# Test loads issued by GpSimd, and stores of weight sums and loads of down weights some steps later, in a two-layer FNet and GLU kernel

## The chip, the cores and the metric

The kernel runs on one core of a Trainium2 chip. The metric is the device time of one launch in microseconds. The core's engines work side by side, each through its own instructions in order: TensorE (PE in the profile; its weight loads are PEld), VectorE (DVE), ScalarE (ACT), GpSimd (POOL) and SyncE (SP), which here only issues transfers between the chip's memory (HBM) and the core's on-chip memory (SBUF).

## The reference

Two layers; each adds a Fourier mixing of the normalized rows and then a gated unit (GLU) of the normalized rows. x is 2048 rows of 640; the gate and up weights are 640 x 1728, the down weights 1728 x 640; all float32.

```python
def _A_ref(x, dft_seq_re, dft_seq_im, dft_hid_re, dft_hid_im):
    a = jnp.einsum("bsd,ed->bse", x, dft_hid_re)
    b = jnp.einsum("bsd,ed->bse", x, dft_hid_im)
    y = jnp.einsum("ts,bse->bte", dft_seq_re, a) - jnp.einsum("ts,bse->bte", dft_seq_im, b)
    return y

def _B_ref(x, w_gate, w_up, w_down):
    g = jnp.einsum("bsd,df->bsf", x, w_gate)
    u = jnp.einsum("bsd,df->bsf", x, w_up)
    h = _sigmoid(g) * u
    return jnp.einsum("bsf,fd->bsd", h, w_down)

x = A_x
x = x + _A_ref(_layernorm(x, axis=-1), A_dft_seq_re, A_dft_seq_im, A_dft_hid_re, A_dft_hid_im)
x = x + _B_ref(_layernorm(x, axis=-1), B_w_gate, B_w_up, B_w_down)
x = x + _A_ref(_layernorm(x, axis=-1), A_dft_seq_re, A_dft_seq_im, A_dft_hid_re, A_dft_hid_im)
x = x + _B_ref(_layernorm(x, axis=-1), B_w_gate, B_w_up, B_w_down)
```

The four Fourier matrices are inputs.

## The kernel before

**Numbers and memory.** x stays in SBUF, in one big tile (`big`) that also holds everything else. Operands of the matmuls are pairs of float16 parts: a high half, written by ScalarE (`split`, L236), and a low half, what the high half leaves, written by VectorE (L238). A product is three float16 products. Room in `big` is handed out by a planner (`take`) when the program is built; a new tile that lies where an old one lay waits on the chip until the old one has been read.

**Stages.** An opening does the first layer's Fourier mixing, which uses the mirror symmetry of the Fourier matrices. The GLU then takes the 2048 rows in four blocks of 512 (b = 0 to 3), each in steps: 14 steps j = 0 to 13 of gate and up products (13 tiles of 128 columns and a tail), and 8 steps of down products (`down`, L1242).

- Block 0 multiplies straight on (`gate_up`, 30 matmuls of 128x512 a step, L1049). In layer 1 its weights w(0,j) (gate), w(1,j) (up) and w(2,j) (down) arrive from HBM (`load_w`, L954 and L956), are split (`split_w`), and are kept in HBM as float16 pairs (`keep_w`, tensors kept_w, store at L254) for later use. ScalarE takes a step's result by a sigmoid (L1063), VectorE multiplies (L1064) into a tile `hf`, and a step later the result is split into halves (`gated_parts`, L1073 and L1074).
- Blocks 1 to 3 use seven smaller products in place of eight (`seven`, L1095). These need four sums of parts of the gate and up weights, s1 to s4: GpSimd adds them from the raw weights (`make_sums`, L998 to L1001), and `split_sums` makes the halves and stores them (tensors kept_s, through `keep` at L254). For 3 <= j < 13 both tiles of the sums lie in two fixed places that take turns. Later blocks load them with `load_s` (L1020 to L1023).

In layer 1, while block 1 to 3 run, the results of each block are folded for the second layer's mixing: statistics on VectorE (L415, L416), a power and scales on GpSimd (L398 to L411, L606 to L633), whose results ScalarE applies (L621, L623). Also in block 0, VectorE and GpSimd add the last of the mixing to x (`add_hidden`: L940 on VectorE, and one copy on GpSimd, L938).

**Tests.** The shortcuts hold only if the Fourier matrices have the symmetry, so the kernel tests it: beside layer 1's blocks 1 to 3 and layer 2's blocks 0 to 2 it loads all of the matrices in pieces, combines mirrored rows and columns on VectorE (`test_rows`, L1297 to L1300, and its like), and sums the squares of what is left on ScalarE (`square_rest`, L1275). At the end a flag chooses between this result and a general path. Each layer has 42 such tests of the large matrix, 32 of rows with four loads of 128 KB each (`load_rows`, L1291) and 10 of columns with two loads of 256 KB each (`load_cols`, L1308); layer 2 has 8 more of the small one, with two loads each (`load_hidden_rows`, L1351). The pieces use two rooms by turns, so a load waits until the test before last has been squared.

**Order.** The order is written by hand. `at(u, job)` puts a job into step u; the jobs of a step are emitted in order of u ahead of the step's matmuls, and each engine, SyncE's and GpSimd's transfers included, works strictly through what was emitted to it. So an instruction that waits holds up all behind it on its engine. In layer 1 block b starts at step `block[b]` = -3, 19, 41, 63. SyncE issues nearly all transfers and has at most eight under way; only the result's rows are stored by GpSimd (L378). Nothing but the order of emission says which of the waiting stores and loads goes first.

Of the kernel before, what the change touches and what calls it, by code (L numbers as in the profile page):

```python
# [16 lines left out]
P = 128  # L17
S = 2048
D = 640
F = 1728  # L20
NS = S // P
ND = D // P
# [7 lines left out]
HS = S // 2  # L30
# [148 lines left out]
@with_exitstack  # L179
def kernel(ctx: ExitStack, tc: tile.TileContext, x, ct, wh, wg, wu, wc, wd, out):  # L180
    nc = tc.nc
    pool = ctx.enter_context(tc.tile_pool(name="sb", bufs=1))
    psum = ctx.enter_context(tc.tile_pool(name="ps", bufs=1, space=bass.MemoryType.PSUM))
    dram = ctx.enter_context(tc.tile_pool(name="dr", bufs=1, space=bass.MemoryType.DRAM))

    big = pool.tile([P, (UNITS + 2 * CK) * UNIT], F32, name="big")
    acc = [psum.tile([P, 512], F32, name=f"acc{i}") for i in range(6)]
    flag = pool.tile([P, 1], I32, name="flag")
    with tc.manual_schedule():
        folded(ctx, tc, pool, dram, big, acc, flag, x, ct, wh, wg, wu, wc, wd, out)  # L190
    bad = nc.values_load(flag[0:1, 0:1], min_val=0, max_val=1,
                         skip_runtime_bounds_check_because="it is the result of a comparison")
    with tc.If(bad != 0):
        with tc.manual_schedule():
            general(tc, big, [acc[2 * i : 2 * i + 2] for i in range(4)], x, ct, wh, wg, wu, wc, wd, out)


def folded(ctx, tc, pool, dram, big, acc, flag, x, ct, wh, wg, wu, wc, wd, out):
    nc = tc.nc
# [33 lines left out]
    def split(dh, dl, src, s, do=ALL):  # L233

        if 0 in do:
            nc.scalar.activation(dh, src, AF.Copy, scale=s)  # L236
        if 1 in do:
            nc.vector.scalar_tensor_tensor(dl, src, s, dh, op0=OP.mult, op1=OP.subtract)  # L238
# [13 lines left out]
    def keep(v, *key):  # L252
        kept[key] = dram.tile(list(v.shape), F16, name="kept_" + "_".join(map(str, key)))
        nc.sync.dma_start(kept[key], v)  # L254
# [5 lines left out]
    def at(u, f, *a):  # L260
        jobs[max(0, int(u // 1))].append((u, f, a))

    held = {}
# [16 lines left out]
    def drop(*key):  # L280
        s = held.pop(key if len(key) > 1 else key[0])
        if s.span:
            slots.give(s)
# [703 lines left out]
    def take_sums(key, j):  # L987

        if 3 <= j < NF:
            return fixed(XU + XTU + 16 * (j % 2) + 8 * (key == "sp"), 8, key, j)  # L990
        return take(8, key, j)
# [13 lines left out]
    def split_sums(j, do):  # L1005
        v, w = held["sf", j].f32, take_sums("sp", j) if 0 in do else held["sp", j]
        h, l = w.parts
        for c, sign in ((slice(0, 256), -WS), (slice(256, 1024), WS)):
            split(h[:, c], l[:, c], v[:, c], sign, do)
        if 1 not in do:  # L1010
            return
        drop("sf", j)
        keep(w.f16, "s", j)
        if j < 3:
            held["S", j] = held.pop(("sp", j))
        else:
            drop("sp", j)

    def load_s(j):
        nc.sync.dma_start(take(5, "G", j).f16, kept["w", 0, j])  # L1020
# [261 lines left out]
    def room(k, n=CK):  # L1282
        u = UNITS + CK * (k % 2)
        return big[:, u * UNIT : (u + n) * UNIT]

    def load_rows(r, k):

        v = room(k).rearrange("p (g n c) -> p g n c", g=4, n=2)
        s = 1 + 16 * k
        for g, (row, d) in enumerate(((s, 1), (S - s, -1), (HS - s, -1), (HS + s, 1))):  # L1290
            nc.sync.dma_start(v[:, g], bass.AP(ct.tensor, (r * S + row) * S, [[P, NS], [d * S, 16], [1, P]]))  # L1291

    def test_rows(r, k):
        v = room(k)
# [8 lines left out]
    def load_cols(r, i, k):  # L1303

        n, row = (P, START[i]) if i < NB else (1, SB)
        v = room(k).rearrange("p (g c) -> p g c", g=4)[:n]
        for g, t in ((0, 1 + 256 * k), (2, HS - 256 * (k + 1))):
            nc.sync.dma_start(v[:, g : g + 2], bass.AP(ct.tensor, (r * S + row) * S + t, [[2 * S, n], [HS, 2], [1, 256]]))  # L1308

    def test_cols(r, i, k):  # L1310
        v = room(k)[: P if i < NB else 1]
# [35 lines left out]
    def load_hidden_rows(r, k):  # L1347

        v = room(k)[: 20 * ND].rearrange("p (g n c) -> p g n c", g=2, c=P)
        for g, (row, d) in enumerate(((1 + 80 * k, 1), (D - 1 - 80 * k, -1))):  # L1350
            nc.sync.dma_start(v[:, g], bass.AP(wh.tensor, (r * D + row) * D, [[P, ND], [d * D, 80], [1, P]]))  # L1351

    def test_hidden_rows(r, k):
        a, b = (room(k)[: 20 * ND, 4 * P * g : 4 * P * (g + 1)] for g in range(2))
# [112 lines left out]
    for layer in range(2):  # L1467
# [10 lines left out]
        block = []  # L1478
# [23 lines left out]
        if first:  # L1502
            for b in range(NB):
# [12 lines left out]
                else:  # L1516
                    for k in range(2):
                        v = d0 + 4 * k
# [41 lines left out]
        for b in range(1, NB):  # L1560
            for i in range(2):
                u = block[b] - 8 + 1.2 * i
# [9 lines left out]
        for b in range(NB):  # L1572
            for j in range(NF + 1):
                for q in ((0, j), (1, j)) if j < NF else ((3, 0),):
                    u = block[b] + j
# [12 lines left out]
            at(block[0] + j + (1.6 if j > 2 else 1.3), gated_parts, j)  # L1588
        for j in range(NF + 1):
            if first:  # L1590
                at(block[0] + 0.8 * j - 0.5, load_w, 2, j)
                at(block[0] + 0.8 * j + 1.6, split_w, 2, j)
                at(block[0] + j + 4, keep_w, 2, j)
            else:
                at(block[0] + j, load_w_again, 2, j)
                at(block[1] + j - 0.3, test_w, 2, j)

        if first:
            for j in range(NF):
                if 3 <= j < NF:  # L1600
                    u = block[0] + j - 1.5
                else:
                    u = block[1] - 8 + 1.5 * j
                    at(u - 2, load_sums, j)
                at(u, make_sums, j)
                at(u + 1.55, split_sums, j, (0,))
                at(u + 1.9, split_sums, j, (1,))
            at(block[0] + 12, close_slots)


# [2 lines left out]
        else:  # L1613
            u0, u1 = block[0] + 8, block[2] + 14
        tests = [(load_rows, test_rows, (layer, k)) for k in range(2 * NS)]
        tests += [(load_cols, test_cols, (layer, i, k)) for i in range(NB + 1) for k in range(2)]

        pace = (u1 - u0) / len(tests)
        for q, (load, test, key) in enumerate(tests):
            u = u0 + pace * q  # L1620
# [5 lines left out]
        if not first:  # L1626
            tests = [(load_hidden_rows, test_hidden_rows, (r, k), 15.5 + 1.7 * (4 * r + k), 2.8) for r in range(2)
                     for k in range(4)]
            tests += [(load_hidden_cols, test_hidden_cols, (r, j), 29.8 + 0.9 * (3 * r + j), 1.4) for r in range(2)
                      for j in range(3)]  # L1630
            for load, test, key, u, later in tests:
                at(block[2] + u, load, *key)
                at(block[2] + u + later, test, *key)
                at(block[2] + u + 1.15 * later, square_rest)
            at(block[3] + 16, test_all)
# [171 lines left out]
```

## Time and profile before

| | us |
|---|---|
| median of 3 runs | 1168.69 (1167.34 to 1170.28) |
| profiled execution, its own time | 1166.17 |
| its span | 1164.4 |
| TensorE busy in the span | 1128.2 |
| VectorE busy | 738.8 |
| ScalarE busy | 508.0 |
| GpSimd busy | 149.5 |
| mean granted clock of TensorE | 0.995 of full speed |

The span runs from the first to the last instruction; 1.77 us of the profiled execution lie around it. Rows of the profile name a line of the kernel, an engine, an operation and what it writes and reads (out<-in); "x30" counts instructions that stand together, and a bracket such as [1.84 <-DVE big L238] is the idle time ahead of the row and the instruction that ended it. Rows of SPq are transfers as SyncE issues them.

### The profile page before, as it was taken

How to read it: one execution, taken by the hardware profiler on the slowest of the kernel's cores; microseconds unless marked ns; L12 is line 12 of the kernel's file. 1: busy time of each engine (PE TensorE's matmuls, PEld its weight loads, DVE VectorE, ACT ScalarE, POOL GpSimd, SP SyncE). 2: the span in 40 equal slices, each digit the busy share in tenths (PEclk: the TensorE clock that was granted, in tenths of full speed). 3: DMA queues.
4: the chain of work that ended last, by engine and by line, in shares of the span. 5: the costliest groups of instructions: out<-in, count | busy, mean ns of one | idle time of the engine just before them, and what ended most of it. 6: DMA issues, size and time to landing. Idle time of an engine off the chain costs nothing.

```text
span 1164.4 us, 22633 instructions
## 1 busy us (share of the span) xinstructions
PE 1128.2 (97%) x8784; PEld 859.6 (74%) x8784; DVE 738.8 (63%) x1636; ACT 508.0 (44%) x1094; POOL 149.5 (13%) x269
## 2 busy tenths in 40 slices
PE   5699999999999999999999999999999999999997
PEld 2467346788878887888776844678887888788875
DVE  7996698668656776676427566746974557524530
ACT  6865474155524653365304422315552455225420
POOL 2312486110001010100000001000000001000000
PEclk9999999999999999999999999999999999999998
DMA  9417698849595977769305442787849683667301
GB/s 275 138 46 231 228 350 295 240 136 262 160 240 149 263 211 192 220 222 253 94 1 169 169 129 67 197 236 229 253 148 243 223 268 133 139 211 236 121 18 38
DMA packets 225621, 216.40 MB, mean 186 GB/s; under 512 B 68034, under 2 KB 181851, under 8 KB 225502
## 3 DMA queue, kind: packets, MB, share of 16 engines
q1 hardware_dynamic: 224862, 212.23, 61.5%
q0 software_dynamic: 640, 2.62, 0.6%
q8 instruction: 71, 1.16, 0.4%
q14 instruction: 48, 0.39, 0.1%
HBM read 171.03 MB, written 30.40 MB: 173 GB/s over the span
## 4 chain that ended last, share of the span: by engine, by line
PE 93%; DVE 3%; DMA 2%; POOL 1%; SPq 1%; ACT 0%; issue 0%; DVEq 0%; POOLq 0%
PE acc L1095 40%; PE acc L1242 31%; PE acc L1049 14%; PE acc L855 4%; PE acc L1178 2%; PE acc L773 2%; DVE big L238 1%; DMA big<-in_ct 1%; DMA big<-in_x 1%; DMA big<-in_wh 1%; PE acc L523 0%; DMA big<-in_wd 0%; POOL quad L372 0%; DVE big L627 0%; DVE big L664 0%
## 5 line engine op out<-in xcount | busy, mean ns | idle before, releaser
L1095 PE MATMUL acc<-big 128*128 128x256 f16 x4212 | 463.1, 273 | 0.1
L1095 PEld LDWEIGHTS <-big 128*128 128x128 f16 x4212 | 412.0, 98 | 48.6 <-DMA big<-kept_w 0.3
L1242 PE MATMUL acc<-big 128*128 128x320 f16 x2624 | 357.7, 299 | 0.0
L1242 PEld LDWEIGHTS <-big 128*128 128x128 f16 x2624 | 256.7, 98 | 99.7
L1099 ACT ACTIVATE big<-acc 128x256 f32<-128x256 f32 x312 | 116.6, 381 | 208.8 <-PE acc L1095 207.4
L1049 PE MATMUL acc<-big 128*128 128x512 f16 (+1 forms) x990 | 178.1, 342 | 4.6 <-DVE big L238 4.6
L1049 PEld LDWEIGHTS <-big 128*128 128x128 f16 x990 | 96.9, 98 | 84.9 <-DVE big L238 5.6
L1275 ACT ACTIVATE big<-big 128x768 f32<-128x768 f32 (+8 forms) x104 | 79.4, 764 | 124.9 <-DVE big L1300 91.2
L1163 DVE TENSOR_TENSOR big<-big 128x512 f16<-128x512 f32 x78 | 53.8, 690 | 109.2 <-ACT big L1162 109.2
L1257 DVE SCALAR_TENSOR_TENSOR big<-acc,big 128x320 f32<-128x320 f32 x64 | 28.4, 484 | 93.5 <-PE acc L1242 93.4
L238 DVE SCALAR_TENSOR_TENSOR big<-big 128x640 f16<-128x640 f32 (+6 forms) x81 | 64.9, 842 | 0.5 <-ACT big L236 0.4
L1141 ACT ACTIVATE big<-big 128x512 f32<-128x512 f32 x78 | 47.8, 627 | 37.2 <-DVE big L1132 36.9
L1297 DVE TENSOR_TENSOR big<-big 128x256 f32<-128x256 f32 x64 | 26.6, 416 | 49.8 <-DMA big<-in_ct 49.8
L1132 DVE TENSOR_TENSOR big<-big,acc 128x512 f32<-128x512 f32 x78 | 53.1, 681 | 4.2 <-PE acc L1095 4.0
L1151 DVE SCALAR_TENSOR_TENSOR big<-acc,big 128x256 f32<-128x256 f32 x78 | 32.6, 418 | 35.1 <-PE acc L1095 30.8
L236 ACT ACTIVATE big<-big 128x640 f16<-128x640 f32 (+7 forms) x81 | 49.6, 664 | 6.7 <-POOL big L998 4.3
L1162 ACT ACTIVATE big<-big 128x512 f16<-128x512 f32 x78 | 48.8, 625 | 6.5 <-DVE big L1153 5.6
L855 PE MATMUL acc<-big 128*128 128x321 f16 (+3 forms) x324 | 49.0, 300 | 1.1 <-DVE big L238 1.1
L1064 DVE SCALAR_TENSOR_TENSOR big<-acc,big 128x512 f32<-128x512 f32 x26 | 17.9, 687 | 40.4 <-PE acc L1049 28.5
L855 PEld LDWEIGHTS <-big 128*128 128x128 f16 (+3 forms) x324 | 28.2, 95 | 20.3 <-issue 7.7
L509 ACT ACTIVATE big<-big 128x384 f16<-128x384 f32 (+2 forms) x48 | 28.9, 647 | 31.0 <-DVE big L491 26.7
L1063 ACT ACTIVATE big<-acc 128x512 f32<-128x512 f32 x26 | 15.4, 592 | 57.6 <-DVE big L1074 27.2
(183 smaller groups left out, 1001.5 us busy)
## 6 DMA issues: line engine op xcount, KB each, us to landing
big<-kept_w SPq DMA_DIRECT2D x125, 320.0 KB
big<-kept_s SPq DMA_DIRECT2D x75, 512.0 KB
big<-in_ct SPq DMA_DIRECT2D x256, 128.0 KB
big<-kept_w SPq DMA_DIRECT2D x78, 192.0 KB
kept_w<-big SPq DMA_DIRECT2D x41, 320.0 KB
big<-in_ct SPq DMA_DIRECT2D x32, 256.0 KB
kept_s<-big SPq DMA_DIRECT2D x13, 512.0 KB
big<-in_wg SPq DMA_DIRECT2D x16, 320.0 KB
```

The costliest lines, as they stand in the source:

```text
L236: nc.scalar.activation(dh, src, AF.Copy, scale=s)
L238: nc.vector.scalar_tensor_tensor(dl, src, s, dh, op0=OP.mult, op1=OP.subtract)
L855: nc.tensor.matmul(ps[:m, :EC], z[:, at : at + m], w[:, 384 * wp : 384 * wp + EC], start=(d == 0 and zp == HI and wp == HI), stop=(d == ND ...
L1049: nc.tensor.matmul(ps, w[wp][:, d * P : (d + 1) * P], xt[:, xp, :], start=(d == 0 and wp == HI and xp == HI), stop=(d == ND - 1 and wp == LO))
L1095: nc.tensor.matmul(ps, wt, xt, start=start and n == 0, stop=n == len(todo) - 1, skip_group_check=not start)
L1099: nc.scalar.activation(dst, ps, AF.Copy)
L1132: nc.vector.tensor_tensor(v, v, other, op=OP.add)
L1141: nc.scalar.activation(v, v, AF.Sigmoid, scale=SG)
L1162: nc.scalar.activation(s.parts[HI], v, AF.Copy)
L1163: nc.vector.tensor_tensor(s.parts[LO], v, s.parts[HI], op=OP.subtract)
L1242: nc.tensor.matmul(held["pd", e][0][:, :EH], held["ht", j].parts[hp][:, i * P : (i + 1) * P], held["w", 2, j].parts[wp][:, e * EH : (e + 1 ...
L1275: nc.scalar.activation(v, v, AF.Square, accum_out=new_sum()[:p])
```

## The change

Three things are moved.

1. In block 0 of layer 1 the store of a step's weight sums, for j >= 3, leaves `split_sums` (part 1 of it at `block[0] + j + 0.4`) for a job of its own, `keep_sums`, one step later.
2. The down weights of tile j are loaded at `block[0] + 0.75 j + 2.2` instead of `0.8 j - 0.5`, split at `0.75 j + 4.2` instead of `0.8 j + 1.6`, and stored at `j + 5.5` instead of `j + 4`.
3. The loads of the symmetry tests of rows and columns, 312 transfers in both layers (2 x 32 x 4, 2 x 10 x 2 and 8 x 2), are issued by GpSimd instead of SyncE.

```diff
@@ split_sums
         drop("sf", j)
-        keep(w.f16, "s", j)
         if j < 3:
             held["S", j] = held.pop(("sp", j))
-        else:
-            drop("sp", j)
+            keep(w.f16, "s", j)
+
+    def keep_sums(j):
+        keep(held["sp", j].f16, "s", j)
+        drop("sp", j)
@@ load_rows
         for g, (row, d) in enumerate(((s, 1), (S - s, -1), (HS - s, -1), (HS + s, 1))):
-            nc.sync.dma_start(v[:, g], bass.AP(ct.tensor, (r * S + row) * S, [[P, NS], [d * S, 16], [1, P]]))
+            nc.gpsimd.dma_start(v[:, g], bass.AP(ct.tensor, (r * S + row) * S, [[P, NS], [d * S, 16], [1, P]]))
@@ load_cols
-            nc.sync.dma_start(v[:, g : g + 2], bass.AP(ct.tensor, (r * S + row) * S + t, [[2 * S, n], [HS, 2], [1, 256]]))
+            nc.gpsimd.dma_start(v[:, g : g + 2], bass.AP(ct.tensor, (r * S + row) * S + t, [[2 * S, n], [HS, 2], [1, 256]]))
@@ load_hidden_rows
-            nc.sync.dma_start(v[:, g], bass.AP(wh.tensor, (r * D + row) * D, [[P, ND], [d * D, 80], [1, P]]))
+            nc.gpsimd.dma_start(v[:, g], bass.AP(wh.tensor, (r * D + row) * D, [[P, ND], [d * D, 80], [1, P]]))
@@ the schedule
             if first:
-                at(block[0] + 0.8 * j - 0.5, load_w, 2, j)
-                at(block[0] + 0.8 * j + 1.6, split_w, 2, j)
-                at(block[0] + j + 4, keep_w, 2, j)
+                at(block[0] + 0.75 * j + 2.2, load_w, 2, j)
+                at(block[0] + 0.75 * j + 4.2, split_w, 2, j)
+                at(block[0] + j + 5.5, keep_w, 2, j)
...
                 at(u, make_sums, j)
                 at(u + 1.55, split_sums, j, (0,))
                 at(u + 1.9, split_sums, j, (1,))
+                if j > 2:
+                    at(u + 2.9, keep_sums, j)
```

Behind the new function the line numbers grow by two: L1064 is L1066 after, L1074 is L1076, L1291 is L1293.

How the order changes, at three places. SyncE in block 0 of layer 1, before, where step j=3 ends and j=4 begins. kept_w_0_3 is the store of the gate weights of j=3, kept_w_1_3 of its up weights, kept_w_2_0 of the first down weights, kept_s_3 that of the sums of j=3; the numbers behind are only those of the tensors.

```order
L956 DMA big_63<-in_wd 128x640 x5
L254 DMA kept_s_3_1174<-big_63 128x2048
L956 DMA big_63<-in_wd 128x640
L254 DMA kept_w_0_3_1196<-big_63 128x1280
L254 DMA kept_w_1_3_1213<-big_63 128x1280
L954 DMA big_63<-in_wg 128x640
L954 DMA big_63<-in_wu 128x640
L254 DMA kept_w_2_0_1223<-big_63 128x1280
L956 DMA big_63<-in_wd 128x640
L254 DMA kept_s_4_1237<-big_63 128x2048
```

And the same place after the change.

```order
L956 DMA big_63<-in_wd 128x640 x3
L254 DMA kept_w_0_3_1185<-big_63 128x1280
L254 DMA kept_w_1_3_1202<-big_63 128x1280
L954 DMA big_63<-in_wg 128x640
L954 DMA big_63<-in_wu 128x640
L254 DMA kept_s_3_1221<-big_63 128x2048
L956 DMA big_63<-in_wd 128x640
L254 DMA kept_w_0_4_1250<-big_63 128x1280
L254 DMA kept_w_1_4_1267<-big_63 128x1280
```

The store of the sums of j=3 stands behind the two stores of the weights of j=3 and the next two weight loads, where it stood ahead of them; fewer down weights are loaded ahead.

VectorE at the same steps, before: L920 and L927 belong to the mixing, the pairs of L238 with 128x640 are the low halves of w(0,j) and w(1,j), single ones those of down weights, and 128x256 with 128x768 those of the sums.

```order
L238 SCALAR_TENSOR_TENSOR big<-big 128x640 x2
L1074 TENSOR_TENSOR big<-big 128x512 x2
L238 SCALAR_TENSOR_TENSOR big<-big 128x640 x2
L927 TENSOR_TENSOR big<-big 128x642
L238 SCALAR_TENSOR_TENSOR big<-big 128x640
L1074 TENSOR_TENSOR big<-big 128x512
L238 SCALAR_TENSOR_TENSOR big<-big 128x256
L238 SCALAR_TENSOR_TENSOR big<-big 128x768
L1064 SCALAR_TENSOR_TENSOR big<-acc_346,big 128x512
L238 SCALAR_TENSOR_TENSOR big<-big 128x640 x2
```

After, from the same pair of weight splits, that of j=5, to that of j=6:

```order
L238 SCALAR_TENSOR_TENSOR big<-big 128x640 x2
L1076 TENSOR_TENSOR big<-big 128x512 x2
L927 TENSOR_TENSOR big<-big 128x642
L1076 TENSOR_TENSOR big<-big 128x512
L238 SCALAR_TENSOR_TENSOR big<-big 128x256
L238 SCALAR_TENSOR_TENSOR big<-big 128x768
L1066 SCALAR_TENSOR_TENSOR big<-acc_346,big 128x512
L238 SCALAR_TENSOR_TENSOR big<-big 128x640 x2
```

The three splits of down weights between the gated halves and the sums are gone from here; the first down split now comes behind the pair of j=6.

GpSimd in layer 1, before, where the first block's folding ends (coef, L661) and the powers of the next rows begin (L398):

```order
L610 TENSOR_TENSOR coef_88<-quad_76 128x2
L661 MEMSET big 128x4
L398 TENSOR_SCALAR small_85<-small_85 128x2
L399 TENSOR_TENSOR small_85<-small_85,half 128x2
L403 TENSOR_TENSOR small_85<-small_85 128x2
```

After the change:

```order
L610 TENSOR_TENSOR coef_88<-quad_76 128x2
L661 MEMSET big 128x4
L1293 DMA big<-in_ct 128x2x128 x20
L398 TENSOR_SCALAR small_85<-small_85 128x2
L399 TENSOR_TENSOR small_85<-small_85,half 128x2
```

Twenty test loads, each of which waits for its room, stand ahead of the powers on GpSimd's queue; further on there are 4, and then 36, ahead of the next ones.

## The prediction

> **What bounds the kernel now.** I read the page first: the shares of the chain of work that ended last, then the costliest groups, whose last column is the idle time just before a group and what ended it.
>
> ```profile
> PE 93%; DVE 3%; DMA 2%; POOL 1%; SPq 1%; ACT 0%; issue 0%; DVEq 0%; POOLq 0%
> L1095 PE MATMUL acc<-big 128*128 128x256 f16 x4212 | 463.1, 273 | 0.1
> L1242 PE MATMUL acc<-big 128*128 128x320 f16 x2624 | 357.7, 299 | 0.0
> L1049 PE MATMUL acc<-big 128*128 128x512 f16 (+1 forms) x990 | 178.1, 342 | 4.6 <-DVE big L238 4.6
> ```
>
> TensorE is the bound: 93% of that chain, and its two great groups (the seven products, L1095, and the down products, L1242) stand idle 0.1 and 0.0 us. Whatever leaves it work to do costs nothing. Behind the opening there is one thing to win: 4.6 us before the straight gate and up products of block 0, L1049, released by the low half of a weight split, DVE L238. TensorE's own timeline says where, and shows a third wait, of the opening, for comparison; under it the windows (time; busy PE, PEld, DVE, ACT, POOL; granted clock, DMA share, GB/s).
>
> ```profile
> 42.02 7.53 PE L773 MATMUL acc<-big 128*128 128x256 f16 x52 [2.67 <-DVE big L664]
> 137.87 6.65 PE L1049 MATMUL acc<-big 128*128 128x512 f16 x30 [1.84 <-DVE big L238]
> 147.31 3.20 PE L1049 MATMUL acc<-big 128*128 128x512 f16 x9 [2.80 <-DVE big L238]
> ...
> 40.00:44.00 4.00, 1.98 (x11) 1.63 (x12) 3.79 (x11) 3.77 (x8) 0.30 (x5) 0.80 0.00 0
> 129.00:148.00 19.00, 14.36 (x67) 6.19 (x66) 16.05 (x24) 10.12 (x18) 10.14 (x10) 1.00 0.68 243
> 148.00:152.00 4.00, 4.00 (x12) 1.48 (x11) 4.00 (x7) 2.58 (x5) 3.59 (x2) 0.57 0.74 253
> ```
>
> TensorE waits 1.84 us for the weights of j=7 and 2.80 us for those of j=8. A step of 30 matmuls takes 6.65 us. Behind the longer wait the granted clock is 0.57 over 4 us, which loses (1 - 0.57) x 4 = 1.72 us; around the shorter one it is 1.00; the 2.67 us wait at 42 us also stands in a window below full clock (0.80). So the longer wait costs twice. The Trainium skill ("TensorE: Matmul & The Clock Gate", Part 1, What's actually happening) puts the fall to half clock behind a whole idle window of some 3.4 us; by it 2.80 us would not do, the fall would have another cause and stay, and the sum below would be 4.64 and not 6.36. I go by the rows, where the two waits above 2.6 us show the fall and the one of 1.84 us does not.
>
> Why is VectorE late? The timeline, 20 us earlier:
>
> ```profile
> 118.23 1.29 DVE L238 SCALAR_TENSOR_TENSOR big<-big 128x256 f16<-128x256 f32 x2
> ...
> 119.58 0.33 SPq L254 DMA_DIRECT2D kept_s<-big  x1
> ...
> 120.43 1.31 SPq L254 DMA_DIRECT2D kept_w<-big  x2
> ...
> 125.47 0.60 ACT L1063 ACTIVATE big<-acc 128x512 f32<-128x512 f32 x1 [11.06 <-DMA kept_w<-big]
> ...
> 126.10 0.69 DVE L1064 SCALAR_TENSOR_TENSOR big<-acc,big 128x512 f32<-128x512 f32 x1 [6.59 <-ACT big L1063]
> 126.73 1.56 DVE L238 SCALAR_TENSOR_TENSOR big<-big 128x640 f16<-128x640 f32 x2
> ```
>
> The weight sums of j=3 are split on VectorE until 119.5. Their store (kept_s) is next in SyncE's queue, which is strictly in order, so the stores of gate and up weights of j=3 (kept_w) leave only at 120.43. The sigmoid of j=3 writes on memory that the second of them still reads, and waits 11.06 us; VectorE then waits 6.59 us for the sigmoid, and everything behind it, the splits of w(6), w(7), w(8) among it, is as much later.
>
> **The change, part by part.** *1. The store of sums a step later.* By the order, the kept_w of j=3 now stand right behind three loads of down weights; nothing late is ahead of them. They no longer wait for anything of VectorE's late work, and the sigmoid can run when TensorE has done j=3, at 136.0 (the start of j=7 without its wait, below) less 3 x 6.65, so 116.1, instead of 125.5. *2. Down weights later.* Three splits of them leave the stretch before w(6): 0.82 us each. Worked through by hand for VectorE in its new order, from 112.0, where w(5) starts, with the durations of these rows:
>
> ```profile
> 112.01 1.55 DVE L238 SCALAR_TENSOR_TENSOR big<-big 128x640 f16<-128x640 f32 x2
> 113.48 1.29 DVE L1074 TENSOR_TENSOR big<-big 128x512 f16<-128x512 f32 x2
> ...
> 116.89 0.82 DVE L238 SCALAR_TENSOR_TENSOR big<-big 128x640 f16<-128x640 f32 x1
> 117.62 0.69 DVE L1074 TENSOR_TENSOR big<-big 128x512 f16<-128x512 f32 x1
> ...
> 118.78 1.32 POOL L998 TENSOR_TENSOR big<-big 128x256 f32<-128x256 f32 x1 [21.38 <-DVE big L238]
> ...
> 121.66 0.72 POOL L1001 TENSOR_TENSOR big<-big 128x256 f32<-128x256 f32 x1
> ...
> 128.21 0.89 DVE L940 TENSOR_TENSOR big<-big 128x321 f32<-128x321 f32 x2
> ...
> 129.23 0.71 POOL L938 COPY big<-big 1x642 f32<-1x642 f32 x1 [6.85 <-PE acc L1049]
> 129.97 0.90 DVE L940 TENSOR_TENSOR big<-big 128x321 f32<-128x321 f32 x2 [0.88 <-POOL big L938]
> ...
> 132.02 1.37 POOL L998 TENSOR_TENSOR big<-big 128x256 f32<-128x256 f32 x1 [2.08 <-DVE big L238]
> ...
> 135.87 1.19 POOL L1001 TENSOR_TENSOR big<-big 128x256 f32<-128x256 f32 x1
> ```
>
> w(5), low halves of j=0 and 1, join (0.82 as well), low half of j=2, sums of j=3: 112.0 + 1.55 + 1.29 + 0.82 + 0.69 + 1.29 = 117.6. Gate of j=3 0.69 and w(6) 1.56: 119.9. Adds of the spectral part 0.89: 120.8. The second adds wait for GpSimd's copy L938, which follows its weight sums of j=5; a set of four took 3.6 us (118.78 to 122.38) and, later, 5.0 (132.02 to 137.06). At 3.6 the copy ends at 121.9, and the adds at 122.8. First down split, sums of j=4, low half, join, second down split, gate of j=4, together 5.13: 128.0. w(7): **129.5** (at 5.0 a set, 131.0). TensorE, without its wait, wants it at 137.87 - 1.84 = 136.0: 5.0 to 6.5 us to spare. On to w(8), with 0.78 for its first half: sums of j=5, adds, the copy behind two more sets, then 0.90 + 0.69 + 0.82 + 0.69 + 0.78: **139.0** at 3.6 a set, **141.9** at 5.0. TensorE wants it at 136.0 + 6.65 = 142.7: 0.8 to 3.7 us to spare. Past that a step without adds is 0.69 + 1.29 + 0.82 + 0.69 + 1.56 = 5.05 us of VectorE to 6.65 of TensorE, so the lead grows. Both waits go, and with the longer one the clock's fall: 1.84 + 2.80 + 1.72 = **6.36 us**.
>
> What is late next: TensorE reaches block 0's down products 6.36 us sooner.
>
> ```profile
> 184.19 42.00 PE L1242 MATMUL acc<-big 128*128 128x320 f16 x308
> ...
> 186.15 0.63 ACT L1073 ACTIVATE big<-big 128x512 f16<-128x512 f32 x1 [3.84 <-DMA kept_w<-big]
> ...
> 191.72 1.20 DVE L1229 TENSOR_TENSOR big<-big 64x512 f16<-64x512 f32 x1 [0.69 <-ACT big L1227]
> ```
>
> The tail of the gated rows is ready at 192.9; TensorE uses it at the end of the second group of down products, some 10.5 us after 184.2 (42.00 / 308 a matmul: 78 of them), 194.8. To spare now: 1.9; so the tail has to come 4.4 us sooner or take back what is missing. The 3.84 us before L1073 is the same kind of wait (a kept_w behind a kept_s) and goes by the same edit, and the 6.59 us of VectorE go too; against it stand three or four down splits moved behind (2.5 to 3.3 us). I take it to move in full; the other end, not at all, costs 4.4.
>
> *3. The 312 test loads move to GpSimd's queue.* The one row of this trace where GpSimd issues transfers (ns: least, mean, longest), and what the tests wait for now (us in all, times, longest):
>
> ```profile
> L378 POOL DMA_INDIRECT out<-big,rows x8: 960/1138/1588, 767.5 to 1146.1; - x8
> DVE big L1297 <- DMA big<-in_ct: 49.8, 14, 7.8
> ```
>
> SyncE's time that this frees was not on the path: VectorE waits 49.8 us in all for test data, and yet L1095, beside which the tests run, stands idle 0.1. Gain: nothing. The price of a GpSimd issue of 128 KB is not in the trace. The nearest row is 1.14 us; from below 0.96, from above 1.14 stretched by what the same GpSimd add shows beside a busy VectorE (L998: 1.37 at 132, 2.71 at 148 against 0.73 at 196): at 1.37/0.73, 2.1 us, at 2.71/0.73, 4.2.
>
> ```profile
> 148.41 2.71 POOL L998 TENSOR_TENSOR big<-big 128x256 f32<-128x256 f32 x1 [4.75 <-DMA big<-in_wu]
> 195.98 0.73 POOL L998 TENSOR_TENSOR big<-big 128x256 f32<-128x256 f32 x1 [2.47 <-DMA big<-in_wu]
> 228.91 57.64 PE acc L1095 x528
> 354.24 57.64 PE acc L1095 x528
> 359.14 0.84 ACT L1275 ACTIVATE big<-big 128x768 f32<-128x768 f32 x1
> 362.23 0.67 POOL L398 TENSOR_SCALAR quad<-quad 128x4 f32<-128x4 f32 x1 [66.24 <-DVE quad L416]
> 368.37 0.18 POOL L633 TENSOR_TENSOR big<-quad 1x1 f32<-1x1 f32 x1
> 372.76 0.65 ACT L621 ACTIVATE big<-big,coef,quad 128x321 f32<-128x321 f32 x1
> ```
>
> Pace: a block of 22 steps is 354.24 - 228.91 = 125.3 us, 5.70 a step; 42 tests are spread over 51 steps, so 6.9 us a test. A row test has 4 loads: up to 6.9 / 4 = 1.73 us each GpSimd keeps up; at 1.14 it is busy 4.6 of 6.9. Queued behind the loads, which wait for a free room: the fold's scales (L398 to L633). In block 2 four loads are released by the squares at 360.0 to 360.2, take 4.6 us, and the chain of 6.3 us ends at 371, still ahead of its reader at 372.76; up to some 1.6 us a load this costs nothing. I take 1.14, so nothing.
>
> Sum: 6.36 us. The profiled execution, 1166.17 (span 1164.4 and 1.77 around it), would be 1159.8; the median of the runs shown is 2.52 above it, and from it the time is **1162.3**.
>
> **Rivals.** *One wait stays* (the tail does not come sooner, or w(8) loses its 0.8 us, or the clock falls all the same): for it, the small margins at w(8) and the tail; 4.4 given back, 1166.7, or 1.7, 1164.0. *The change doesn't do what it says*: VectorE's work as such (16.05 of 19 us in 129 to 148), not the order, sets the lateness, and the down splits, moved 3 steps, only collide later; against it, the 6.59 us in which it waits: 1168.7. *Slower*: GpSimd can't keep pace. Place: row tests of both layers, 32 each. From 1.73 us a load; at 1.14 x 1.37 / 0.73 = 2.14 us a test takes 8.6 instead of 6.9, VectorE's queue in order waits for it, then the seven products: 1.7 x 64 = 106 us, 1268. For it: L998's stretch; against: eight issues of L378 at 1.59 at most, with VectorE at work beside them. The Trainium skill ("SBUF — State Buffer", SBUF: two separate sides) speaks against the change here: some VectorE operations lock GpSimd out of writing descriptors, so its transfers starve, and it advises issue from SyncE or ScalarE.
>
> **How the numbers follow.** Forecast (both waits and the clock's fall go) 0.61, by itself 1160.5 to 1164.5: the scatter of the three runs, 1.4 and 1.6, and the clock's 1.72. One wait stays 0.15; nothing changes 0.11; slower 0.13. The range 1160 to 1169.5 leaves out the slow rival and little more. With 0.3% (3.5 us, about what a measurement of this kernel can tell), faster is below 1165.2: the forecast and a third of the second case, 0.66; within it 0.21; slower 0.13.
>
> **What would show it.** Right: in the profile after, L1049 with no idle time before it; the clock 1.00 behind 142; the sigmoid of j=3 near 116 without its 11.06 us; down products starting near 178; GpSimd's issues near 1.1 us, and L1095 still idle 0.1. Wrong: a wait before L1242 at some 188 (the tail); idle time before L1095 released by VectorE or ScalarE, with L1297 waiting longer (GpSimd's pace) or L621 waiting for GpSimd (the fold); or L1049's 4.6 unchanged.

## The result and the profile after

| | before | after |
|---|---|---|
| median, us | 1169.36 (1167.34 to 1170.28, 4 runs) | 1161.90 (1158.61 to 1163.32, 4 runs) |
| profiled execution's span, us | 1164.4 | 1156.8 |
| mean granted clock of TensorE | 0.995 | 0.999 |
| GpSimd busy, us | 149.5 | 368.4 |

The ratio of the times is 0.9945, with a 95% interval of 0.9929 to 0.9961: 4.6 to 8.3 us gained, 6.4 in the middle (7.46 between the two medians). The forecast was 1162.3.

The page of the kernel after: the shares of the chain that ended last, and the groups that answer to those of before (busy time, mean ns | idle time before, and what ended it). The line numbers are two higher.

```profile
PE 84%; DMA 2%; ACT 1%; POOL 1%; DVE 0%; issue 0%; SPq 0%; DVEq 0%; POOLq 0%
...
L1097 PE MATMUL acc<-big 128*128 128x256 f16 x4212 | 462.8, 273 | 0.0
...
L1244 PE MATMUL acc<-big 128*128 128x320 f16 x2624 | 357.7, 299 | 0.0
...
L1293 POOL DMA_DIRECT2D big<-in_ct x256 | 175.1, 689 | 232.5 <-DVE big L1302 108.0
...
L1051 PE MATMUL acc<-big 128*128 128x512 f16 (+1 forms) x990 | 176.5, 340 | 0.8 <-ACT big L236 0.5
```

The 4.6 us before the straight products (L1051, before L1049) are down to 0.8, the other groups have no wait, and GpSimd has become busy with test loads without TensorE waiting for it. The chain's share for TensorE is lower because the chain, followed back, takes another way through the opening and block 0; TensorE is busy 97% of the span as before.

The timeline after, in block 0 of layer 1 (start, duration; idle time before and releaser in brackets):

```profile
103.78 1.32 SPq L254 DMA_DIRECT2D kept_w<-big  x2
...
116.29 0.60 ACT L1065 ACTIVATE big<-acc 128x512 f32<-128x512 f32 x1 [3.67 <-PE acc L1051]
...
117.31 0.68 DVE L1066 SCALAR_TENSOR_TENSOR big<-acc,big 128x512 f32<-128x512 f32 x1
117.45 0.33 SPq L254 DMA_DIRECT2D kept_s<-big  x1
...
130.18 2.75 DVE L238 SCALAR_TENSOR_TENSOR big<-big 128x640 f16<-128x640 f32 x4
...
139.61 3.49 DVE L238 SCALAR_TENSOR_TENSOR big<-big 128x640 f16<-128x640 f32 x5
...
173.78 0.60 ACT L1065 ACTIVATE big<-acc 128x512 f32<-128x512 f32 x1 [2.43 <-POOL big L1000]
174.28 1.76 ACT L236 ACTIVATE big<-big 128x640 f16<-128x640 f32 x3
...
175.06 0.61 PE L1051 MATMUL acc<-big 128*128 128x512 f16 x2 [0.53 <-ACT big L236]
...
175.92 2.98 PE L1051 MATMUL acc<-big 128*128 128x512 f16 x13 [0.25 <-DVE big L238]
```

The stores of w(3) leave at 103.78, the sigmoid of j=3 runs at 116.29, released by TensorE and no longer by a store, and the low halves of w(7) and w(8) start at 130.18 and 139.61, ahead of TensorE's need. What is left is new: at the end of block 0 a sigmoid waits 2.43 us for GpSimd's weight sums, the split of the tail's weights (L236) comes behind it, and TensorE waits 0.53 and 0.25 us. The sigmoid reads nothing that GpSimd writes, only the product; so what it waits for must be room, a place in `big` where the sums still read the raw weights.

Where the 7.6 us of the two spans lie is read from the chain of before and after: the start of block 0's down products, that of the last down products, and the last instruction.

```profile
184.35 44.55 PE acc L1242 x328
...
1111.64 44.57 PE acc L1242 x328
...
1156.23 0.49 DVE big L1257
```

```profile
178.90 44.55 PE acc L1244 x328
...
1105.82 44.57 PE acc L1244 x328
...
1150.41 0.49 DVE big L1259
```

Up to block 0's down products 5.45 us are gained; from there to the last ones 0.37 more; and from the end of the last instruction to the end of the span, in which only the last store is still under way, it is 7.7 us before (1164.4 - 1156.72) and 5.9 after (1156.8 - 1150.90): 1.8 us that no instruction shows. The first of these was forecast. The second and third were not, and the experiments ask which part of the change each comes from.

### The profile page after: what moved, and what is told of

Same layout as the page of the kernel before. It is cut to its first block, busy times and chain, and to the rows that moved or that the text cites. A ratio compares the mean times of both kernels' runs of the same rounds, so it can differ in the third digit from the quotient of the medians.

```text
span 1156.8 us, 22767 instructions
## 1 busy us (share of the span) xinstructions
PE 1127.3 (97%) x8784; PEld 860.0 (74%) x8784; DVE 738.5 (64%) x1636; ACT 507.7 (44%) x1094; POOL 368.4 (32%) x581
## 3 DMA queue, kind: packets, MB, share of 16 engines
q1 hardware_dynamic: 140014, 166.97, 49.8%
## 4 chain that ended last, share of the span: by engine, by line
PE 84%; DMA 2%; ACT 1%; POOL 1%; DVE 0%; issue 0%; SPq 0%; DVEq 0%; POOLq 0%
PE acc L1097 40%; PE acc L1244 31%; PE acc L1051 8%; PE acc L855 2%; PE acc L1180 2%; PE acc L773 1%; DMA kept_s<-big 1%; DMA kept_w<-big 1%; ACT big L236 1%; DVE big L238 0%; POOL big L1001 0%; PE acc L523 0%; ACT big L479 0%; ACT big L480 0%; POOL big L999 0%
## 5 line engine op out<-in xcount | busy, mean ns | idle before, releaser
L1244 PE MATMUL acc<-big 128*128 128x320 f16 x2624 | 357.7, 299 | 0.0
L1244 PEld LDWEIGHTS <-big 128*128 128x128 f16 x2624 | 256.7, 98 | 99.7
L1293 POOL DMA_DIRECT2D big<-in_ct x256 | 175.1, 689 | 232.5 <-DVE big L1302 108.0
L1101 ACT ACTIVATE big<-acc 128x256 f32<-128x256 f32 x312 | 116.1, 381 | 208.9 <-PE acc L1097 207.5
L1051 PE MATMUL acc<-big 128*128 128x512 f16 (+1 forms) x990 | 176.5, 340 | 0.8 <-ACT big L236 0.5
L1051 PEld LDWEIGHTS <-big 128*128 128x128 f16 x990 | 96.5, 98 | 79.8 <-ACT big L236 1.0
L238 DVE SCALAR_TENSOR_TENSOR big<-big 128x640 f16<-128x640 f32 (+6 forms) x81 | 64.4, 833 | 2.9 <-ACT big L236 2.3
L236 ACT ACTIVATE big<-big 128x640 f16<-128x640 f32 (+7 forms) x81 | 50.7, 665 | 16.6 <-POOL big L1001 5.3
L1310 POOL DMA_DIRECT2D big<-in_ct x40 | 27.3, 686 | 94.9 <-ACT big L1277 47.3
L1299 DVE TENSOR_TENSOR big<-big 128x256 f32<-128x256 f32 x64 | 26.6, 416 | 36.8 <-DMA big<-in_ct 36.8
L1300 DVE TENSOR_TENSOR big<-big 128x256 f32<-128x256 f32 x64 | 26.9, 421 | 30.9 <-DMA big<-in_ct 30.9
```

Source lines behind the costliest of these rows:

```text
L1051: nc.tensor.matmul(ps, w[wp][:, d * P : (d + 1) * P], xt[:, xp, :], start=(d == 0 and wp == HI and xp == HI), stop=(d == ND - 1 and wp == LO))
L1101: nc.scalar.activation(dst, ps, AF.Copy)
L1244: nc.tensor.matmul(held["pd", e][0][:, :EH], held["ht", j].parts[hp][:, i * P : (i + 1) * P], held["w", 2, j].parts[wp][:, e * EH : (e + 1 ...
L1293: nc.gpsimd.dma_start(v[:, g], bass.AP(ct.tensor, (r * S + row) * S, [[P, NS], [d * S, 16], [1, P]]))
```

## The experiments

In the table, the median and the ratio to before (its 95% interval), and from the profile the start of block 0's down products and TensorE's waits in block 0 behind 97 us. Rows between lines ran side by side on one chip.

| kernel | median us | ratio | down products start | waits |
|---|---|---|---|---|
| before | 1166.33 | | 184.35 (first profile) | 4.6 |
| later down weights alone | 1171.92 | 1.0049 [1.0036, 1.0062] | 184.25, with 3.6 us of waits in them | 4.4 |
| store of sums later alone | 1158.99 | 0.9944 [0.9931, 0.9957] | 177.78 | 0 |
| GpSimd's loads alone | 1164.00 | 0.9985 [0.9975, 0.9994] | 182.58 | 4.7 |
| change without GpSimd's loads | 1164.87 | 0.9984 [0.9975, 0.9994] | 180.69 | 2.5 |
| --- second set, before 1167.50 | | | | |
| store of sums and GpSimd's loads | 1159.30 | 0.9922 [0.9902, 0.9942] | 180.73 | 0.2 |
| whole change | 1160.92 | 0.9941 [0.9919, 0.9963] | 178.91 | 1.0 |
| whole, store half a step sooner | 1163.13 | 0.9956 [0.9939, 0.9973] | 183.38 | 3.4 |
| whole, row loads cut in four | 1348.41 | 1.1544 [1.1511, 1.1578] | 178.71 | 0.8 |
| --- third set, before 1165.79 | | | | |
| store of sums later alone | 1160.04 | 0.9950 [0.9937, 0.9963] | 178.27 | 0 |
| store of sums and GpSimd's loads | 1157.73 | 0.9933 [0.9920, 0.9946] | 177.65 | 0 |
| change without GpSimd's loads | 1164.29 | 0.9983 [0.9972, 0.9994] | 179.03 | 0.6 |
| whole change | 1162.05 | 0.9964 [0.9952, 0.9976] | 183.93 | 2.8 |

### The down weights alone

To the kernel before only this is done:

```diff
-                at(block[0] + 0.8 * j - 0.5, load_w, 2, j)
-                at(block[0] + 0.8 * j + 1.6, split_w, 2, j)
-                at(block[0] + j + 4, keep_w, 2, j)
+                at(block[0] + 0.75 * j + 2.2, load_w, 2, j)
+                at(block[0] + 0.75 * j + 4.2, split_w, 2, j)
+                at(block[0] + j + 5.5, keep_w, 2, j)
```

> Only the down weights are loaded, split and stored later; the store of weight sums stays ahead of the stores of the same step's weights, and SyncE loads the test pieces. My theory (the store of sums in SyncE's queue is what makes everything late): the sums of j=3 are now split at about 117.4 instead of 119.5, so the stores of w(3) leave at some 118.4 instead of 120.4 and the sigmoid of j=3 still waits, until about 123; TensorE still waits before j=7 or j=8, 1 to 3 us in all; the down products of block 0 start between 180.5 and 183 (before 184.35, with the whole change 178.90), 1 to 4 us gained. Rival (VectorE's work, not the order of stores): the three splits that leave the stretch bring it all, start at 179, 5 us or more gained.

It is slower, by 5.6 us, and its down products start no sooner than before (184.25), which neither reading had. Its timeline, ScalarE, VectorE and TensorE:

```profile
123.64 0.60 ACT L1063 ACTIVATE big<-acc 128x512 f32<-128x512 f32 x1 [10.72 <-DMA kept_w<-big]
...
145.50 33.50 PE L1049 MATMUL acc<-big 128*128 128x512 f16 x148 [2.61 <-DVE big L238]
180.57 0.60 PE L1049 MATMUL acc<-big 128*128 128x512 f16 x2 [1.57 <-ACT big L236]
...
190.21 0.63 ACT L1073 ACTIVATE big<-big 128x512 f16<-128x512 f32 x1 [5.37 <-DMA kept_w<-big]
...
195.16 1.34 DVE L238 SCALAR_TENSOR_TENSOR big<-big 128x640 f16<-128x640 f32 x1
195.30 0.45 PE L1242 MATMUL acc<-big 128*128 128x320 f16 x2 [0.56 <-DVE big L1074]
...
198.75 1.57 PE L1242 MATMUL acc<-big 128*128 128x320 f16 x8 [3.01 <-DVE big L1229]
```

The sigmoid of j=3 still waits, until 123.64, as my theory had it (about 123), and the wait before j=7 is gone, that before j=8 still 2.61. But the gain does not last: at the end of block 0 the store of weights is again what ScalarE waits for (5.37 us), down splits now stand there on VectorE, and the tail of the gated rows comes 3.01 us late for the down products. This is the rival of the prediction in which the tail doesn't come sooner (4.4 us there), here with 3.01 us. The rival of the experiment (VectorE's work) has fallen too: with that work moved away most of the waits are there.

### The store of sums alone

To the kernel before only `keep_sums` is added; down weights and SyncE's test loads are as they were.

```diff
-        keep(w.f16, "s", j)
...
+    def keep_sums(j):
+        keep(held["sp", j].f16, "s", j)
+        drop("sp", j)
...
+                if j > 2:
+                    at(u + 2.9, keep_sums, j)
```

> Only the store of weight sums comes a step later; down weights as before, and SyncE loads the test pieces. My theory: the stores of w(3) no longer wait for VectorE's sums, the sigmoid of j=3 runs before 122 instead of 125.5, and most of the gain is there: down products of block 0 from 178.9 to 181, 3.5 to 5.5 us gained. What could spoil it: six loads of down weights stand ahead of these stores, and the last waits for room that a split frees at about 116. Rival (VectorE's work sets it): start of the down products at 183 or later, at most 1.5 us gained.

Its timeline, TensorE and ScalarE:

```profile
96.77 81.00 PE L1051 MATMUL acc<-big 128*128 128x256 f16 x431
...
119.50 0.60 ACT L1065 ACTIVATE big<-acc 128x512 f32<-128x512 f32 x1 [5.18 <-DMA kept_w<-big]
...
177.62 22.58 PE L1244 MATMUL acc<-big 128*128 128x320 f16 x165
```

The sigmoid of j=3 still waits for its store, behind six loads of down weights, but only until 119.50, and that is enough: TensorE runs from 96.77 into the down products without a wait. This one part gives 6.6 us to block 0 (184.35 to 177.78), more than the whole change does (5.45) and than my theory had (3.5 to 5.5), and the time is 7.3 us below before.

### GpSimd's loads alone

```diff
-            nc.sync.dma_start(v[:, g], ...)
+            nc.gpsimd.dma_start(v[:, g], ...)
```

(the same in all three loads, to the kernel before)

> Only the 312 test loads move to GpSimd. My theory: nothing in block 0, down products of block 0 start at 184.35 within 0.2 with both waits (1.84 and 2.80 us) as before; later at most 0.4 us gained, since the seven products of blocks 1 and 2 took 71.57 and 71.55 us before and 71.45 and 71.40 with the whole change; whole time within 1 us of before. Rival (GpSimd's queue brings a part of the gain, or costs what the other parts bring in): more than 2 us either way.

It is 2.3 us faster by the medians (0.7 to 2.9 by the interval of the ratio): more than the 1 us of my theory, and by the medians what the rival had, which began at 2. TensorE's timeline and a window (busy PE, PEld, DVE, ACT, POOL; granted clock, DMA share, GB/s):

```profile
137.77 6.65 PE L1049 MATMUL acc<-big 128*128 128x512 f16 x30 [1.90 <-DVE big L238]
147.22 2.98 PE L1049 MATMUL acc<-big 128*128 128x512 f16 x13 [2.81 <-DVE big L238]
```

```profile
148.00:152.00 4.00, 4.00 (x21) 1.78 (x19) 4.00 (x7) 2.50 (x5) 3.68 (x2) 1.00 0.69 221
```

Block 0 has both waits as before, and yet its down products start 1.77 us sooner: behind the same wait of 2.8 us the clock stayed at 1.00, where the profile of before had 0.57. So one and the same wait, of one length and in the same instructions, brought a fall in one execution and none in another. The 2.3 us of the medians are another matter, below.

### The change without GpSimd's loads

> The whole change but for the test loads, which stay with SyncE. My theory: down products of block 0 start at 178.9 as with the whole change, 5.4 to 5.8 us gained in all; the 0.1 us a block that the seven products of blocks 1 and 2 gain is gone. Rival: without GpSimd's loads less than half of the gain stays.

Only 1.5 us by the medians (0.16% by the ratio) are left of the gain, not 5.4 to 5.8, and TensorE waits 2.5 us in block 0, and 1.7 us in blocks 1 and 2 together. The rival had it right that less than half stays; the next two sets ask why.

### GpSimd's loads with the store of sums

> The store of weight sums a step later and the test loads on GpSimd, but the down weights as before. Theory now: the store of sums brings the whole gain, the later down weights take 1 to 3 us of it back in block 0, and GpSimd's loads only free SyncE's queue for the weights of blocks 1 and 2. Then the down products of block 0 start at 177.8 as with the store of sums alone, no wait of TensorE is left behind 97 us, and the time is that of the store of sums alone within 1 us, 2 to 4 us below the whole change. Rival (the later down weights help when the other two parts are there): the time is that of the whole change or more.

By the medians the time is within 0.3 us of the store of sums alone, as my theory had it. But that run (1158.99) stands in the other set, beside a before of 1166.33, where before is 1167.50 here; by the ratios this version is 0.0022 lower, some 2.6 us, and only the third set compares the two on one chip. It is 1.6 us below the whole change, where the theory had 2 to 4. The start at 180.73 is 3 us late for another reason: the clock fell in this execution's opening (0.79, 0.50, 0.50 and 0.93 in four windows from 48 to 64 us, behind a wait of 1.94), and block 0 began 2.7 us later; in it there is one wait of 0.15.

### The whole change again

> The whole change once more, beside the others on one chip. Up to the end of block 0 it has the same instructions as the version without GpSimd's loads, which started block 0's down products at 180.69 where the profile of the whole change had 178.90. If the difference is one of executions, the start lies anywhere from 178.5 to 181 here; if GpSimd's loads act on block 0, it is again 178.90 within 0.3. Time 5 to 7 us below before.

178.91, as the second reading had it: GpSimd's loads would seem to act on block 0. The third set speaks against it: there the start is 183.93 with them and 179.03 without.

### The store of sums half a step sooner

```diff
-                if j > 2:
-                    at(u + 2.9, keep_sums, j)
+                if j > 2:
+                    at(u + 2.5, keep_sums, j)
...
-                            at(u - 4, load_w, *q)
+                            at(u - 3.95, load_w, *q)
```

> The whole change, with the store of sums moved half a step back, so that it stands behind the stores of its step's weights but ahead of the next loads of gate and up weights, which wait for GpSimd's sums. Theory: what is left of waits in block 0 comes from ScalarE's sums waiting for the store of the sums two steps before (4.3 us in the profile of the whole change); with the store sooner, that wait is below 2 us and the down products of block 0 start at 178.0 to 178.5. Rival (the bunched down weights at the end of block 0 cause what is left): start not before 178.7.

The loads of the gate and up weights go a twentieth of a step back, so that the store stands ahead of them. It is not better: 2.2 us slower than the whole change by the medians, a start at 183.38 with 3.4 us of waits, and the clock falls here too, in the windows around and behind a wait of 1.68 us:

```profile
177.85 0.61 PE L1051 MATMUL acc<-big 128*128 128x512 f16 x2 [1.68 <-ACT big L236]
```

```profile
176.00:180.00 4.00, 2.06 (x8) 0.63 (x8) 2.79 (x5) 3.42 (x7) 3.43 (x8) 0.90 1.00 353
180.00:184.00 4.00, 4.00 (x16) 1.78 (x15) 4.00 (x7) 2.64 (x5) 3.44 (x8) 0.67 1.03 414
```

The wait at which this was aimed is gone (no row of ScalarE waits for kept_s in block 0 any more), but a sigmoid now waits 4.13 us for GpSimd's sums, beside the 2.43 us that stay. So my theory of what was left is refuted as a way to gain: the place of that store isn't what holds the end of block 0.

### Row loads cut in four

```diff
-            nc.gpsimd.dma_start(v[:, g], bass.AP(ct.tensor, (r * S + row) * S, [[P, NS], [d * S, 16], [1, P]]))
+            for n in range(4):
+                nc.gpsimd.dma_start(v[:, g, n // 2, 64 * (n % 2) : 64 * (n % 2 + 1)],
+                                    bass.AP(ct.tensor, (r * S + row + n // 2 * d) * S + 64 * (n % 2),
+                                            [[P, NS], [2 * d * S, 8], [1, 64]]))
```

> The whole change, with each load of a row test cut into four: 16 GpSimd transfers of 32 KB a test instead of 4 of 128 KB, the same bytes, in 128 pieces of 256 B instead of 256 pieces of 512 B. If a GpSimd transfer costs much the same whatever its size (0.6 us and more), a test takes 16 x 0.6 = 9.6 us of GpSimd against the pace of 6.9, VectorE waits for it and TensorE with it: 2.7 x 64 = 170 us slower than the whole change. If the cost goes with the pieces (0.34 us each), 5.4 us a test stay below the pace, and the time is within 3 us of the whole change.

Slower by 187 us (1348.41 - 1160.92). GpSimd's issues of the whole change and of this kernel (least, median, longest ns), and what TensorE waits for here (us in all, times, longest):

```profile
L1293 POOL DMA_DIRECT2D big<-in_ct x256: 681/681/1009, 244.8 to 908.9; - x128
```

```profile
L1294 POOL DMA_DIRECT2D big<-in_ct x1024: 517/593/1057, 244.6 to 1102.3; - x171
...
PE acc L1097 <- ACT big L1101: 137.6, 21, 21.1
```

A transfer of a quarter of the size costs 0.59 us against 0.68: nearly a fixed price. With it, a row test takes 16 x 0.593 = 9.5 us of GpSimd at a pace of 6.9, and (9.5 - 6.9) x 64 = 166 us. The run gave 187, and in part by another way: TensorE is busy 1165.6 us here against 1127.3, at a mean granted clock of 0.94. So the slow rival of the prediction is a real mechanism of this kernel, with about the point at which it decides: at four loads of 0.68 the change stands at 2.7 of 6.9 us, far on the safe side.

### Four versions side by side

All have the store of sums a step later; with and without the later down weights, with and without GpSimd's loads.

> First of four versions run on one chip, all with the store of sums a step later: with or without the later down weights, with or without GpSimd's loads. This one has neither. Theory: it is the fastest or ties with the fastest; no wait of TensorE between 97 us and the end of block 2; 7 us or more below before.

> Store of sums and GpSimd's loads, down weights as before. Theory: within 1.5 us of the version without GpSimd's loads, since no wait is left that they could end. Rival (GpSimd's loads bring something of their own, as the 1.8 us of their run alone might say): 1.8 us or more below it.

> Store of sums and later down weights, SyncE loads the test pieces. Theory: 4 to 6 us above the version with the store of sums alone; part of it in block 0 (its down products started 2.9 us later in the first look), part in the seven products of blocks 1 and 2, which wait for weights queued behind test loads on SyncE (2.1 us in the first look). If the start of block 0's down products is 178.9 now, the first look's 180.7 was that execution's; if it is 180.7 again, SyncE's loads reach back into block 0 in a way that the order doesn't show.

> The whole change. Theory: 1 to 2 us above the versions without the later down weights (block 0's down products at 178.9 against 177.8), and 2 to 5 us below the version without GpSimd's loads, because those take the test loads out of the queue in which the weights of blocks 1 and 2 stand. Rival (the later down weights are what GpSimd's loads need): the whole change is the fastest of the four.

The later down weights cost 4.25 us with SyncE's loads (1164.29 - 1160.04) and 4.32 with GpSimd's (1162.05 - 1157.73). GpSimd's loads gain 2.31 without them and 2.24 with them, and 2.33 alone in the first set; each is a difference of medians of 5 to 12 runs, and the intervals of the ratios overlap a little. As far as they tell, the two parts do not depend on each other; my theory, that GpSimd's loads repair what the later down weights do to SyncE's queue and bring at most 1.5 us without them, has fallen, and the rival that the later down weights are what GpSimd's loads need with it. In the profiles, the change without GpSimd's loads now starts its down products at 179.03, and the whole change at 183.93:

```profile
175.19 0.61 PE L1051 MATMUL acc<-big 128*128 128x512 f16 x2 [0.32 <-ACT big L236]
```

```profile
171.34 0.60 PE L1051 MATMUL acc<-big 128*128 128x512 f16 x2 [2.16 <-ACT big L236]
```

```profile
172.00:176.00 4.00, 3.57 (x10) 1.37 (x11) 3.34 (x6) 3.97 (x9) 1.12 (x3) 0.63 0.96 337
```

(first the one, then the other, and the other's window behind its wait.) Both have the same instructions up to there, so what differs is the execution; 0.8 us of it lie ahead of block 0 (TensorE's long row begins at 96.85 in the first and at 97.64 in the second). Of six profiles with the store of sums in its place and the later down weights, the loads cut in four among them, TensorE's waits in block 0 are 0.6, 0.8, 0.8, 1.0, 2.5 and 2.8 us; of four with the store of sums but not the later down weights they are 0, 0, 0 and 0.2. One row parts the two groups without exception: the sigmoid near the end of block 0 waits 2.42 or 2.43 us for GpSimd's sums (L1000) in all eight profiles with later down weights, that of the down weights alone among them, and in none of the six others. First the whole change, then the version without later down weights, both of this set:

```profile
178.82 0.60 ACT L1065 ACTIVATE big<-acc 128x512 f32<-128x512 f32 x1 [2.43 <-POOL big L1000]
```

```profile
171.58 0.57 ACT L1065 ACTIVATE big<-acc 128x512 f32<-128x512 f32 x1
```

So later down weights leave block 0 without slack at its end: 0.6 to 1.0 us of waits in four of the six profiles, 2.5 in the fifth, and in the sixth a wait of 2.16 us and a fall of the clock behind it. That the 4.3 us of the medians come from executions like the last two is not shown, since only one execution of each run was profiled. What speaks for it: the profiled time less the start of block 0's down products is 979.7 to 980.8 us in all seven profiles with GpSimd's loads of 128 KB, whether they start at 177.65 or at 183.93. So what these executions differ by, they lose ahead of the down products.

GpSimd's 2.3 us are in part the landing of the last store. From the last instruction's end to the end of the span it is 5.9 us in the profile of the whole change and 5.9 to 6.1 in all eight profiles with GpSimd's loads; without them it is 5.9 and 6.0 in the two with the store of sums alone, and 7.7 to 8.1 in the other four (before among them). Those two are the quickest executions of their runs, so without GpSimd's loads the landing may go by the execution; but the profile at 8.0 of the change without GpSimd's loads in the third set is the quickest of its run too, and it stays undecided. Why the last store, which SyncE issues in all of them and over 90 us behind the last of the moved test loads, should land sooner, is open.

**The fastest version** is the store of sums with GpSimd's loads and the down weights as before: 1157.73 against 1162.05 for the whole change in the same set, and 0.9933 [0.9920, 0.9946] of before.

## Why the prediction was right, and where it was not

The time came out at 0.4 us from the forecast, by a sum whose terms did not all hold.

- *The store of sums.* Right, and shown alone: with it no TensorE wait is left in block 0. The sigmoid ran at 116.29 (forecast 116.1); w(7) was split by some 131.7 (VectorE's row from 130.18; forecast 129.5 to 131.0, so a little late) and w(8)'s first half by 140.4 (139.0 to 141.9).
- *Later down weights.* Wrong in sign. The step said that three splits leave the stretch before w(6) and that the lead then grows. The splits do leave that stretch, but the store of sums alone needs no such help, and 4.3 us are lost by the medians. Two things were wrong. The lead does not grow as worked out (5.05 us of VectorE to 6.65 of TensorE): that sum had one down split a step, where the new order has four in three, and each row at its shortest. In the profile after, VectorE takes 6.21 us from one step's gated half to the next without a pause, and the row itself 1.21 us instead of 0.69:

```profile
149.23 1.21 DVE L1076 TENSOR_TENSOR big<-big 128x512 f16<-128x512 f32 x1
...
155.44 1.21 DVE L1076 TENSOR_TENSOR big<-big 128x512 f16<-128x512 f32 x1
```

  TensorE's step in turn is nearer 6.4 us (148 matmuls in 33.50 us, 1.7 of them a fall of the clock, in the row of the down weights alone; 30 of them make 6.4). VectorE's steps are as long without the later down weights, 6.2 to 6.5 us in the same stretch, so its pace is not what parts the two. And the prediction asked what is late next only for the tail of the gated rows, and of VectorE, not of the rooms that the moved tiles take: what came is a sigmoid that waits 2.43 us for GpSimd's sums, with TensorE's 0.8 us behind it.
- *The tail of the gated rows* came sooner as taken (no wait before L1244). With the down weights alone it came 3.01 us late, where the other end of that bound was 4.4.
- *The clock's 1.72 us.* The size was right for the execution profiled, the condition (a wait above 2.6 us) was not: waits of 2.81 and 2.43 us ran without a fall, waits of 1.68 and 2.16 with one. A fall costs about as much as taken; whether it comes differs between executions, and fewer waits give it fewer occasions. The Trainium skill's rule ("TensorE: Matmul & The Clock Gate", Part 1, What's actually happening) speaks of a free-running window, which fits falls that come and go behind like waits; that it takes a whole idle window of 3.4 us does not fit the 1.68.
- *GpSimd's loads* were taken as worth nothing at 1.14 us each, from 0.96 to 4.2. Each costs 0.68, below that range, also beside a busy VectorE (64% of the span); the stretched price that the slow rival needed is not there, nor the starving of which the Trainium skill warns ("SBUF — State Buffer", SBUF: two separate sides); whether VectorE runs the operations that this rule means is not shown here. VectorE's two waits for test data (L1299 and L1300, before L1297 and L1298) are 36.8 + 30.9 = 67.7 us after and 49.8 + 16.5 = 66.3 before, so the data come no sooner. Their gain of 2.3 us was not in the sum.

So the measured gain, 6.4 us in the middle of its interval, agrees with the forecast's 6.36 because one step cost what it was to help, and another gave what it was to leave unchanged. That it agrees so closely is luck: by the medians the whole change gained 7.46 us in the first comparison, 6.58 in the second set and 3.74 in the third, where its parts are 5.75 for the store of sums, 4.25 lost by the later down weights and 2.24 gained by GpSimd's loads.

## What to carry to other kernels

A store that waits for late work belongs behind the stores whose memory is needed soon: in an in-order queue of transfers it is the waiting store, not the bytes, that delays the engines. Before crediting a part of a change that moves work later, work through the place where that work arrives, with its own instructions counted in. Try the parts one by one: here one of three brought nearly everything, and another took more than half of it back.

## What the runs showed of the hardware

- An issue by GpSimd costs nearly the same for 128 KB in 256 pieces (0.68 us) and for 32 KB in 128 pieces (0.59 us); cutting transfers is paid nearly in full.
- The fall of the granted clock followed waits of 1.68, 1.94, 2.16, 2.61, 2.67 and 2.80 us and failed to follow others of 2.43 and 2.81; its price was 1.7 us each time in block 0, and 2.7 us of start in the one opening where it reached over four windows of 4 us.
- The last store's landing takes 5.9 to 6.1 us in some profiles and 7.7 to 8.1 in others, without a difference in its own instructions.
